# Inverse-transform tiles placed ahead of the last down products, and a planner's pacing table replaced

## The chip, the cores and the metric

The kernel runs on one core of one Trainium2 chip. Its time is the time of one execution in microseconds (us), as the device reports it. Engines are named as the profile names them: PE (matrix products), PEld (loads of the stationary operand), DVE, ACT, POOL (three elementwise engines) and SP (the queue that issues DMA transfers).

## The reference

The input `x` is 8192 tokens of 448 values. Every token is normalised, and the result is the input plus a spectral branch times a gate:

```python
xn = _layernorm(x, axis=-1)
s = _A_ref(xn, A_w1, A_b1, A_w2, A_b2)
g = _silu(_B_ref(xn, B_w_gate, B_w_up, B_w_down))
return x + s * g
```

`_A_ref` takes a real Fourier transform over the 8192 tokens, sends each frequency through a two-layer complex network in 4 blocks of 112 values (rectifier, soft threshold), and transforms back. `_B_ref` is a gated network: `(gelu(xn @ w_gate) * (xn @ w_up)) @ w_down` with 1792 hidden values.

## The kernel before

**Tiling.** Products are made of 16-bit high and low parts, three products for one, and are collected in PSUM banks (`bx`, `by`, and four shared `bd` banks). A token index is n = 64 n1 + n2, with n1 on the 128 partitions; a chunk is 4 values of n2, 512 tokens, and there are 16 chunks (`NG`), or 32 half chunks. The gated network runs twice over the chunks: pass 0 with hidden tiles 0 to 7, pass 1 with tiles 8 to 13. Pass 0 leaves its part of the down product in DRAM (`prt`), pass 1 adds its own to it. Most down products are made by `down2`, which turns eight block products into seven (`prod2`, numbered 1 to 7) with sums of weight blocks.

**Stages.** Phase 1 normalises, makes the weight parts and does the first stage of the forward transform; phase 2 does the second stage, the spectral network and the first inverse stage by groups of frequencies (`group`); phase 3 does the last inverse stage. The gated network runs beside all three, so PE always has products of both branches to mix. In phase 3 a half chunk `c` needs `u2` (columns of the inverse), `mt` (its matrix), `x2` (the input) and `g2` (the gate, written earlier to `gsp`). `load3` issues these loads on SP, `tiles3` makes the two tiles of 3 matmuls and 448 columns each, DVE multiplies bank and gate, and an addition of `x2` gives the output, which SP stores. For the last two half chunks (c = 30 and 31) the gate is not ready beforehand: their tiles are copied by ACT to `s4` (the profile calls it `s`), and the gate is applied in `ended2` and `last_half`, when the last down products are done: `Silu` on ACT into `th`, times `s4`, plus `x`, then the store. Chunks from `direct` on, except the last, take a middle way (`gate_bank`, `gate`).

**What sets the order.** The order on each engine is fixed when the program is built. The whole kernel is written as small tasks (Python generators); `Pace` advances a clock of its own, gives each instruction a cost on its engine, and starts the task that is next in time. So the order in which instructions stand depends on these costs. On the chip every engine then runs its instructions strictly in that order, waiting on semaphores where a producer on another engine is late.

`STEPS` is the planner's table: from the time in the first column on, the four others are the us added to a DMA's landing, how far ahead an engine may be booked before a task holds back (`clear`), a factor on the costs of all engines but PE, and a bias in the choice between two engines. `Either` makes that choice: `B` is DVE or POOL, `A` is ACT or POOL; the one that would end first by the plan is taken, with the bias added to POOL's end. The costs include that DVE and POOL can hold each other up (`shares`, `push_on`). `END3` is the planner's aim for the end of phase 3: half chunk number k of n3 starts its tiles at t0 + 10 + k (END3 - t0 - 12) / n3.

**What the change touches.** `Pace.note` (L151), which keeps the list of accesses that later instructions must wait for; the additions of `x` in `last_half` and `ended2`, both on DVE (`V`); `END3` in phase 2 and 3; and `STEPS`. All instructions are recorded through one helper, so the profile puts them all at L288.

Of the kernel before, what the change touches and what calls it, by code (L numbers as in the profile page):

```python
# [22 lines left out]
NG = 16  # L23
# [19 lines left out]
STEPS = ((0, 2.75, 0.05, 0.97, 0.0), (15, 2.75, 0.05, 0.97, 0.0), (25, 2.75, 0.05, 1.0, 0.3), (35, 2.75, 0.05, 1.0, 0.3), (45, 2.75, 0.05, 1.07, 0.0), (55, 2.75, 0.05, 1.07, 0.0), (65, 2.75, 0.05, 0.97, 0.0), (75, 2.75, 0.05, 0.97, 0.0), (87, 2.75, 0.15, 1.01, 0.0), (100, 2.75, 0.15, 1.01, 0.0), (125, 2.5, 0.15, 1.04, 0.0), (150, 2.5, 0.15, 1.04, 0.0), (175, 2.5, 0.15, 1.04, 0.0), (200, 2.5, 0.15, 1.04, 0.0), (225, 3.0, 0.15, 0.98, 0.0), (250, 2.75, 0.05, 1.0, 0.0), (275, 2.75, 0.05, 1.0, 0.0), (300, 2.75, 0.05, 1.0, 0.0), (325, 2.5, 0.05, 1.02, 0.0), (350, 2.5, 0.05, 1.02, 0.0), (375, 2.5, 0.05, 1.04, -0.3), (400, 2.5, 0.05, 1.04, -0.3), (425, 2.5, 0.05, 1.04, -0.3), (450, 2.5, 0.05, 1.04, -0.3), (475, 2.5, 0.05, 1.04, -0.3), (500, 2.5, 0.05, 1.04, -0.3), (525, 2.5, 0.05, 1.04, -0.3), (550, 2.5, 0.05, 1.04, -0.3), (575, 3.5, 0.05, 1.0, 0.0), (600, 3.5, 0.05, 1.0, 0.0), (625, 3.5, 0.05, 1.04, 0.0), (650, 3.5, 0.05, 1.04, 0.0), (675, 3.5, 0.05, 1.04, 0.0), (700, 3.5, 0.05, 1.04, 0.0), (725, 2.75, 0.05, 1.0, 0.0), (750, 2.75, 0.05, 1.0, 0.0), (775, 3.0, 0.05, 1.0, -0.3), (800, 3.0, 0.05, 1.0, -0.3), (825, 3.0, 0.05, 1.0, -0.5), (850, 3.0, 0.05, 1.0, -0.5), (875, 3.0, 0.05, 1.0, -0.5), (900, 3.0, 0.05, 1.0, -0.5), (925, 2.75, 0.05, 1.06, 0.0), (950, 2.75, 0.05, 1.06, 0.0), (975, 2.75, 0.05, 1.06, 0.0), (1000, 2.75, 0.05, 1.06, 0.0), (1025, 2.75, 0.05, 1.06, 0.0), (1050, 2.75, 0.05, 1.06, 0.0), (1075, 2.75, 0.05, 1.06, 0.1), (1100, 2.75, 0.05, 1.06, 0.1), (1125, 2.75, 0.05, 1.02, 0.0), (1150, 2.75, 0.05, 1.02, 0.0), (1175, 1.75, 0.05, 1.025, 0.0), (1200, 1.75, 0.05, 1.025, 0.0), (1225, 1.75, 0.05, 1.055, 0.0), (1250, 1.75, 0.05, 1.055, 0.0), (1275, 1.75, 0.05, 1.025, -0.2), (1300, 1.75, 0.05, 1.025, -0.2), (1325, 1.75, 0.05, 1.025, -0.2), (1350, 1.75, 0.05, 1.025, -0.2), (1375, 1.75, 0.05, 1.025, -0.4), (1400, 1.75, 0.05, 1.025, -0.4), (1425, 2.25, 0.1, 1.025, -0.4), (1450, 2.25, 0.1, 1.025, -0.4), (1475, 2.25, 0.1, 1.025, -0.4), (1500, 2.25, 0.1, 1.025, -0.4), (1525, 2.25, 0.1, 1.025, -0.4), (1550, 2.25, 0.1, 1.025, -0.4), (1575, 1.75, 0.1, 1.025, -0.4), (1600, 1.75, 0.1, 1.025, -0.4), (1625, 1.75, 0.1, 1.025, -0.4), (1650, 1.75, 0.1, 1.025, -0.4), (1675, 2.75, 0.05, 0.94, 0.1), (1700, 2.75, 0.05, 0.94, 0.1), (1725, 2.75, 0.05, 0.94, 0.4))  # L43
# [15 lines left out]
class Pace:  # L59
# [90 lines left out]
    def note(self, ap, write, t, e):  # L150
        name, lo, hi = self.region(ap)  # L151
        was = self.seen.setdefault(name, [])
        if write:
            was[:] = [x for x in was if not (lo <= x[0] and x[1] <= hi)]
        was.append([lo, hi, write, t, e])
        return was[-1]
# [399 lines left out]
def afno_geglu_kernel(ctx, tc, x, gu, raw, wd, mlp, b1, b2, c_m, c_mt, c_small, c_rows, out):  # L556
# [1222 lines left out]
    def last_half(i, qq, e, tf, a):  # L1779
# [13 lines left out]
        V.tensor_tensor(th, th, x4, op=ALU.add)  # L1793
# [3 lines left out]
    def ended2(p, i, qq, b, R, earlier=None):  # L1797
# [43 lines left out]
        V.tensor_tensor(th, th, x4, op=ALU.add)  # L1841
# [507 lines left out]
    def stores():  # L2349

        for g, (j0, m) in enumerate(GROUPS):
# [13 lines left out]

            pace.spawn(store())

    END1, END2, END3 = T1 + NG * DT + 12.0, 1450.0, 1730.0

    def phase2():  # L2370
        yield ev("phase1")
# [457 lines left out]
```

## Time and profile before

| | us |
|---|---|
| median of 3 runs | 1739.8 (1739.71 to 1740.24) |
| the profiled execution: its time | 1737.31 |
| its span, first to last instruction | 1735.5 |
| PE busy | 1709.6 of the span |
| DVE, ACT, POOL busy | 1404.9, 1097.0, 937.6 |
| start of PE's last matmuls (21 in 4.13 us) | 1721.74 |
| last DMA issue | 1731.80 |

In the rows of the profile, `bd<-u,mt` is a tile of the last inverse stage; `bd<-dw,h`, `bd<-wt,h`, `bd<-dw,wt` and the same into `by` or `bx` are down products; `g<-bd,ms,g` multiplies a bank and a gate, `g<-g,x` adds the input. A row of a timeline has the start, the time to the end, engine, line, operation, operands and count; in brackets stands the idle time of the engine before it and what ended it. A row of groups has the sum of busy time and the mean of one in ns. Matmuls overlap in the pipeline: 12 of 224 columns take 1.31 us together, though one alone is shown with about 0.26 us.

### The profile page before, as it was taken

Reading aid. Unit: us, or ns where it says so; the run is one execution under the profiler, and the core shown is the slowest. Engines: PE = TensorE matmul, PEld = TensorE weight load, DVE = VectorE, ACT = ScalarE, POOL = GpSimd, SP = SyncE. Lnnn points to the kernel's source line nnn. Section 1 sums busy time; section 2 is a strip of 40 time slices with the busy share of each in tenths; the row PEclk is TensorE's granted clock in tenths of the full one; section 3 lists DMA queues with packets and bytes.
Section 4 is the critical chain, followed back from the end, with each engine's and each line's share of the span. In section 5 each row is a group of like instructions: output and inputs, shape, how many; then the busy total and the mean of one; then the engine's idle time right before and its main releaser. Section 6 shows DMA issues by size and latency. Waiting matters only on the chain.

```text
span 1735.5 us, 40997 instructions
## 1 busy us (share of the span) xinstructions
PE 1709.6 (99%) x15654; PEld 1434.6 (83%) x15654; DVE 1404.9 (81%) x2438; ACT 1097.0 (63%) x2240; POOL 937.6 (54%) x1291
## 2 busy tenths in 40 slices
PE   9999999999999999999999999999999999999997
PEld 4447677766777999998989999999999999889886
DVE  8999888878885778778777788888888787687787
ACT  6767666757675556678776667666766676333333
POOL 3467666667565574457566454355445454344442
PEclk9999999999999999999999999999999999999999
DMA  7448987878858543254346865544556455999987
GB/s 265 149 135 252 270 254 221 288 206 229 237 163 242 149 124 74 60 127 106 92 111 185 210 163 131 120 120 104 131 139 145 113 134 113 293 287 306 303 288 257
DMA packets 438310, 316.63 MB, mean 182 GB/s; under 512 B 305793, under 2 KB 409601, under 8 KB 436321
## 3 DMA queue, kind: packets, MB, share of 16 engines
q1 hardware_dynamic: 437824, 313.99, 64.6%
q8 instruction: 122, 2.00, 0.5%
q14 instruction: 76, 0.61, 0.1%
q10 hardware_dynamic: 288, 0.03, 0.0%
HBM read 137.93 MB, written 108.25 MB: 142 GB/s over the span
## 4 chain that ended last, share of the span: by engine, by line
PE 44%; DVE 3%; POOL 2%; ACT 1%; issue 1%; SPq 0%; DMA 0%; DVEq 0%; ACTq 0%; POOLq 0%
PE bd L288 19%; PE bx L288 14%; PE by L288 11%; DVE wt L288 1%; DVE th L288 0%; POOL wn L288 0%; POOL h L288 0%; DVE va L288 0%; POOL wt L288 0%; DVE h L288 0%; SPq L288 0%; DVE g L288 0%; ACT h L288 0%; DVE o L288 0%; DVE t L288 0%
## 5 line engine op out<-in xcount | busy, mean ns | idle before, releaser
L288 PEld LDWEIGHTS <-wt 128*128 128x128 f16 x9142 | 884.6, 98 | 160.3 <-issue 9.5
L288 PE MATMUL bx<-xta,wt 128*128 128x256 f16 (+1 forms) x2819 | 354.7, 275 | 2.2 <-ACT by L288 1.3
L288 PEld LDWEIGHTS <-h 128*128 128x128 f16 x2711 | 259.6, 98 | 76.3 <-POOL h L288 1.1
L288 PE MATMUL by<-xtb,wt 128*128 128x256 f16 x2080 | 255.2, 273 | 0.6 <-DVE by L288 0.6
L288 PE MATMUL bd<-dw,h 128*128 128x448 f16 (+1 forms) x1536 | 241.3, 306 | 0.4 <-DVE ysb L288 0.4
L288 POOL TENSOR_TENSOR wt<-wt 128x256 f32<-128x256 f32 x133 | 107.2, 806 | 158.8 <-DVE wt L288 151.5
L288 PE MATMUL bx<-xtb,wt 128*128 128x256 f16 x1248 | 153.3, 273 | 0.0
L288 PE MATMUL by<-xta,wt 128*128 128x256 f16 (+1 forms) x899 | 123.9, 282 | 0.7 <-DVE u L288 0.5
L288 DVE TENSOR_TENSOR by<-bx,u 128x512 f32<-128x512 f32 x104 | 72.2, 695 | 40.4 <-PE bx L288 34.8
L288 ACT ACTIVATE u<-by,fc 128x512 f32<-128x512 f32 (+1 forms) x118 | 73.4, 635 | 49.1 <-PE by L288 47.4
L288 PE MATMUL bx<-left,wt 128*128 128x256 f16 x816 | 99.9, 273 | 1.0 <-ACT by L288 1.0
L288 PE MATMUL bd<-dw,wt 128*128 128x224 f16 (+1 forms) x816 | 97.9, 264 | 1.4 <-DVE left L288 1.4
L288 POOL TENSOR_TENSOR t<-h 112x256 f32<-112x256 f32 (+1 forms) x34 | 26.0, 765 | 125.8 <-ACT h L288 104.9
L288 ACT COPY u<-by 128x512 f32<-128x512 f32 x104 | 60.7, 584 | 49.2 <-PE by L288 49.1
L288 ACT CAST h<-wt 128x512 f16<-128x512 f32 (+1 forms) x128 | 68.4, 535 | 34.0 <-DVE wt L288 28.9
L288 DVE SCALAR_TENSOR_TENSOR left<-bd,ms,left 128x448 f32<-128x448 f32 x96 | 64.3, 680 | 27.1 <-PE bd L288 26.6
L288 DVE TENSOR_TENSOR v<-bx,u 128x512 f32<-128x512 f32 x104 | 71.2, 685 | 16.6 <-PE bx L288 15.9
L288 POOL TENSOR_TENSOR h<-wt,h 128x256 f16<-128x256 f32 (+1 forms) x65 | 71.4, 1106 | 15.5 <-ACT h L288 15.4
L288 PE MATMUL bd<-w2t,wn 113*128 113x112 f16 (+1 forms) x1152 | 78.3, 212 | 0.9 <-DVE bd L288 0.6
L288 ACT COPY by<-bx 128x512 f32<-128x512 f32 x104 | 60.0, 577 | 24.8 <-PE bx L288 24.3
L288 PE MATMUL bd<-wt,h 128*128 128x224 f16 x603 | 72.9, 259 | 0.6 <-POOL h L288 0.5
L288 PEld LDWEIGHTS <-wn 113*128 113x128 f16 (+1 forms) x1152 | 69.3, 97 | 4.1 <-issue 1.2
(280 smaller groups left out, 3801.8 us busy)
## 6 DMA issues: line engine op xcount, KB each, us to landing
xts<-sx SPq DMA_DIRECT2D x32, 480.0 KB, 4.1
x<-in_x SPq DMA_DIRECT2D x17, 896.0 KB, 6.9
t<-ysb SPq DMA_DIRECT2D x64, 224.0 KB, 3.8
prt<-th SPq DMA_DIRECT2D x64, 224.0 KB, 3.3
vt<-va SPq DMA_DIRECT2D x256, 56.0 KB, 2.1
left<-prt SPq DMA_DIRECT2D x64, 224.0 KB, 3.8
u<-t SPq DMA_DIRECT2D x32, 448.0 KB, 6.0
x<-in_x SPq DMA_DIRECT2D x32, 448.0 KB, 6.4
```

The costliest lines, as they stand in the source:

```text
L288: return self.pace.issue(self.name, kind, out, ins, lambda: fn(out, *args, **kw))
```

## The change

Four edits. `STEPS` is another table of 75 rows. `END3` goes from 1730 to 1716, so the last half chunks are planned up to 14 us earlier. The additions of `x` in `last_half` and `ended2` go to DVE or POOL, whichever ends first by the plan. And `note` drops an older read of the same stretch by PE when PE reads it again.

```diff
-STEPS = ((0, 2.75, 0.05, 0.97, 0.0), (15, 2.75, 0.05, 0.97, 0.0), (25, 2.75, 0.05, 1.0, 0.3),
+STEPS = ((0, 2.75, 0.05, 1.0, 0.0), (15, 2.75, 0.05, 1.0, 0.0), (25, 2.75, 0.3, 1.0, 0.8),
...
         if write:
             was[:] = [x for x in was if not (lo <= x[0] and x[1] <= hi)]
+        elif e == "PE":
+            was[:] = [x for x in was if x[4] != e or x[2] or x[0] != lo or x[1] != hi]
         was.append([lo, hi, write, t, e])
...
-        V.tensor_tensor(th, th, x4, op=ALU.add)
+        B.tensor_add(th, th, x4)
         yield
         Q.dma_start(blk(ov[:, CH * i:CH * i + CH, :], *qq)[:, v], th)
...
-        V.tensor_tensor(th, th, x4, op=ALU.add)
+        B.tensor_add(th, th, x4)
         PT.put(q)
...
-    END1, END2, END3 = T1 + NG * DT + 12.0, 1450.0, 1730.0
+    END1, END2, END3 = T1 + NG * DT + 12.0, 1450.0, 1716.0
```

Both programs have the same 15654 matmuls, of the same shapes, and the same number and shapes of DMAs; their order differs, and 44 elementwise instructions more stand on POOL, 42 fewer on DVE and 2 fewer on ACT. Of the instructions `wt<-wt,wt` (128x512), for example, DVE had 42 and POOL 22, and now they have 28 and 36. The helper's line is L290 in the changed kernel.

**The end of PE's list.** The last down product is the one into `bx`. Before, seven tiles of the inverse (each 3 matmuls, shown by one) stand behind it: `u_24554` and `u_24606` are half chunks 30 and 31, `u_24325` and `u_24503` two earlier ones.

```order
L288 MATMUL bx<-wt_80,h 128x224
...
L288 MATMUL bd_66<-u_24554,mt 128x448
...
L288 MATMUL bd_69<-u_24325,mt 128x448
...
L288 MATMUL bd_67<-u_24554,mt 128x448
...
L288 MATMUL bd_66<-u_24606,mt 128x448
...
L288 MATMUL bd_69<-u_24606,mt 128x448
...
L288 MATMUL bd_67<-u_24503,mt 128x448
...
L288 MATMUL bd_66<-u_24503,mt 128x448
```

Now `u_24528` and `u_24575` are half chunks 30 and 31, and `u_24345` is the last of the others; the rows from product 6 of `down2` on (`bd_69<-wt_78,h`), one row for each run of equal kind:

```order
L290 MATMUL bd_67<-u_24236,mt 128x448
...
L290 MATMUL bd_66<-u_24528,mt 128x448
...
L290 MATMUL bd_67<-u_24528,mt 128x448
...
L290 MATMUL bd_69<-wt_78,h 128x224
...
L290 MATMUL bd_66<-u_24575,mt 128x448
...
L290 MATMUL bd_67<-u_24575,mt 128x448
...
L290 MATMUL bd_66<-u_24345,mt 128x448
...
L290 MATMUL bd_69<-wt_80,h 128x224
...
L290 MATMUL bx<-wt_80,h 128x224
...
L290 MATMUL bd_67<-u_24345,mt 128x448
```

Six of the seven tiles have moved in among the last down products, three of them in one run ahead of the end of product 6; one stays behind the last down product.

**The end of the elementwise lists.** Before, DVE's last rows, from the addition of the last half down product (`left<-bx`) on; POOL has one addition (`g_24551`) in this stretch, and none behind it:

```order
L288 SCALAR_TENSOR_TENSOR left<-bx,ms,left 128x224
L288 SCALAR_TENSOR_TENSOR g_24551<-bd_69,ms,g_24551 128x448
L288 TENSOR_TENSOR g_24551<-g_24551,x_24507 128x448
L288 TENSOR_TENSOR th<-th,s_21491 128x448
L288 TENSOR_TENSOR th<-th,x_24209 128x448
...
L288 SCALAR_TENSOR_TENSOR g_24683<-bd_67,ms,g_24683 128x448
...
L288 TENSOR_TENSOR th<-th,x_24558 128x224
L288 TENSOR_TENSOR g_24683<-g_24683,x_24610 128x448
...
L288 SCALAR_TENSOR_TENSOR g_24683<-bd_66,ms,g_24683 128x448
```

Now DVE's rows from the same addition on, and then POOL's last ones:

```order
L290 SCALAR_TENSOR_TENSOR left<-bx,ms,left 128x224
L290 TENSOR_TENSOR th<-th,s_21492 128x448
L290 TENSOR_TENSOR th<-th,s_21492 128x224
L290 SCALAR_TENSOR_TENSOR g_24581<-bd_67,ms,g_24581 128x448
L290 TENSOR_TENSOR g_24581<-g_24581,x_24579 128x448
```

```order
L290 TENSOR_TENSOR th<-th,x_24532 128x448
L290 TENSOR_TENSOR g_24581<-g_24581,x_24579 128x448
L290 TENSOR_TENSOR th<-th,x_24240 128x448
L290 TENSOR_TENSOR th<-th,x_24532 128x224 x2
```

Behind `left<-bx` DVE had 16 instructions and now has five (the product `th<-th,s` of 128x224 stands there twice, with `g_24581<-bd_67` between); four of the five additions into `th` at the end have gone to POOL.

**DVE in phase 1.** Here DVE frees the bank `by` for PE with `u<-by,fc,u`. Before, the rows between two of these instructions, and then now:

```order
L288 SCALAR_TENSOR_TENSOR dw_85<-xtb,fd,dw_84 128x448
L288 SCALAR_TENSOR_TENSOR raws<-raws,rowc 128x128
L288 BN_STATS st<-x_411 128x6
L288 BN_AGGR st<-st 128x2
L288 SCALAR_TENSOR_TENSOR dw_85<-wo,fd,dw_84 128x448
L288 SCALAR_TENSOR_TENSOR u_992<-by,fc,u_992 128x512
```

```order
L290 SCALAR_TENSOR_TENSOR dw_85<-xtb,fd,dw_84 128x448
L290 SCALAR_TENSOR_TENSOR raws<-raws,rowc 128x128
L290 SCALAR_TENSOR_TENSOR u_988<-by,fc,u_988 128x512
L290 BN_STATS st<-x_401 128x6
L290 BN_AGGR st<-st 128x2
L290 SCALAR_TENSOR_TENSOR dw_85<-wo,fd,dw_84 128x448
```

A pair of statistics and one `dw` have moved from ahead of `u` to behind it.

2 lines of the change are left out of this document (1 added, 1 removed).

## The prediction, made before the changed kernel ran

> **What bounds the kernel now.** The page comes first: the share of each engine.
>
> ```profile
> span 1735.5 us, 40997 instructions
> PE 1709.6 (99%) x15654; PEld 1434.6 (83%) x15654; DVE 1404.9 (81%) x2438; ACT 1097.0 (63%) x2240; POOL 937.6 (54%) x1291
> ```
>
> PE is busy for all but 26 us of the span, and both programs have the same 15654 matmuls, so the change can only act on those 26 us. The view by windows tells where they lie; of its 21 rows, those with 2 us or more of idle PE, three of the last stage, and the sum.
>
> ```profile
> 0.00:100.00 100.00, 95.10 (x483) 45.04 (x484) 89.22 (x177) 64.33 (x138) 43.32 (x68) 1.00 0.52 183
> 100.00:200.00 100.00, 97.79 (x640) 62.19 (x639) 91.45 (x174) 73.49 (x151) 73.36 (x130) 1.00 0.80 230
> 200.00:300.00 100.00, 97.59 (x770) 74.73 (x769) 88.85 (x153) 67.89 (x135) 65.82 (x115) 1.00 0.83 249
> 800.00:900.00 100.00, 97.61 (x1045) 89.70 (x1044) 79.60 (x129) 75.19 (x164) 67.26 (x78) 1.00 0.47 111
> 1600.00:1650.00 50.00, 50.00 (x457) 44.09 (x456) 37.13 (x53) 18.95 (x34) 21.67 (x25) 1.00 0.98 314
> 1650.00:1700.00 50.00, 49.95 (x458) 44.32 (x457) 40.57 (x59) 18.89 (x33) 21.71 (x22) 1.00 0.91 298
> 1700.00:1736.00 36.00, 24.54 (x212) 20.02 (x209) 27.63 (x49) 11.38 (x21) 8.45 (x8) 0.93 0.65 230
> sum 1736.00, PE 1709.56 PEld 1434.59 DVE 1404.88 ACT 1096.98 POOL 937.64; mean PE 81.41 PEld 68.31 DVE 66.90 ACT 52.24 POOL 44.65
> ```
>
> The last 36 us hold 36.00 - 24.54 = 11.5 us without PE; all before them hold 1700 - (1709.56 - 24.54) = 15.0 us, of which 4.9 + 2.2 + 2.4 in the first 300 us. In between PE's granted clock is 1.00 and it hardly waits. So two things are worth reading: the end, and single waits. The end, from PE's, DVE's and SP's timelines:
>
> ```profile
> 1712.63 1.31 PE L288 MATMUL bd<-dw,wt 128*128 128x224 f16 x12 [0.59 <-DVE left L288]
> 1714.59 1.13 PE L288 MATMUL bd<-wt,h 128*128 128x224 f16 x10 [0.46 <-POOL h L288]
> 1716.01 1.31 PE L288 MATMUL bd<-dw,wt 128*128 128x224 f16 x12 [0.29 <-DVE left L288]
> 1721.46 0.45 PE L288 MATMUL bx<-wt,h 128*128 128x224 f16 x3
> 1721.74 4.13 PE L288 MATMUL bd<-u,mt 128*128 128x448 f16 x21
> 1721.95 0.45 DVE L288 SCALAR_TENSOR_TENSOR left<-bx,ms,left 128x224 f32<-128x224 f32 x1 [0.18 <-PE bx L288]
> 1724.88 0.63 DVE L288 TENSOR_TENSOR th<-th,s 128x448 f32<-128x448 f32 x1 [0.46 <-ACT s L288]
> 1730.02 0.68 DVE L288 SCALAR_TENSOR_TENSOR g<-bd,ms,g 128x448 f32<-128x448 f32 x1
> 1731.15 0.62 DVE L288 TENSOR_TENSOR g<-g,x 128x448 f32<-128x448 f32 x1
> 1731.80 0.36 SPq L288 DMA_DIRECT2D out<-g  x1
> ```
>
> The last down product ends at about 1721.9 (1721.46 + 0.45). Behind it PE makes seven tiles until 1725.87 (1721.74 + 4.13). The gate of the last chunk needs four of them (`s`), so its products start at 1724.88 only, and from there DVE runs without a break until 1731.77; the last store is issued at 1731.80 and the span ends 3.7 us after DVE, at 1735.5. **After PE's last matmul come 9.6 us** in which DVE's list is what ends last.
>
> **The change part by part.** The sum is made against the profiled execution, 1737.31 us (span 1735.5 and 1.8 around it), 2.5 us below the median of the runs, 1739.8; I carry that 2.5 over.
>
> *The six tiles.* They are 18 matmuls of (4.13 - 0.35) / 20 = 0.19 us (0.35 is one alone), 3.4 us. They leave the place behind the last down product and stand ahead of it: PE does the same work in total, so its last matmul stays at 1725.87 unless waits change. What moves is DVE: it had 16 instructions behind `left<-bx` and now has five. One tile (0.57 us) stays, so `left<-bx` starts about 0.4 us before PE's last matmul ends, and PE ends 0.74 us after the last down product. DVE then has its 0.45, three `th` products and the two of `g`; the price of the `th` products by width and of the additions on POOL:
>
> ```profile
> L288 DVE TENSOR_TENSOR th<-th,s 128x224 f32<-128x224 f32 x2 | 0.8, 383 | 0.0
> L288 POOL TENSOR_TENSOR th<-th,x 128x448 f32<-128x448 f32 x5 | 6.1, 1212 | 25.2 <-DVE th L288 25.2
> L288 POOL TENSOR_TENSOR wt<-wt 128x256 f32<-128x256 f32 x62 | 50.4, 813 | 80.0 <-DVE wt L288 76.6
> ```
>
> Alone, DVE's five take 0.63 + 0.38 + 0.68 + 0.38 + 0.62 = 2.7 us; from 0.6 us behind the last down product that ends 3.3 us behind it, 2.6 us behind PE, and with the 3.7 us of store 6.3 us: the lower bound. But two of POOL's last three additions, about 0.75 us each at 224 columns (between 1.21 for 448 and 0.81 for 256), and one of 1.2, stand beside them, and DVE and POOL do hold each other up:
>
> ```profile
> 1610.93 1.15 POOL L288 TENSOR_TENSOR wt<-wt,wt 128x512 f16<-128x512 f32 x1
> 1611.03 2.07 DVE L288 TENSOR_TENSOR g<-g,x 128x448 f32<-128x448 f32 x2
> ```
>
> Two additions of 0.62 took 2.07 us on DVE, beginning while POOL was at work: the first waited until POOL was done. If DVE and POOL take turns for all of these, DVE's second `th` product waits for the whole 1.2 of POOL's addition, and the last two 224-wide additions and products wait for each other by about 0.4 more, the rest passing beside `g<-bd`: 1.6 us later, 7.9 us after PE, the upper bound. I take 7.0, about the middle, since both the free runs of DVE at 1724 to 1731 and the held one at 1611 are rows of this stage. **Gain 9.6 - 7.0 = 2.6 us** (1.7 to 3.3).
>
> [...]
>
> *PE's waits ahead of it.* Three waits near the end sum to 0.59 + 0.46 + 0.29 = 1.3 us. Three tiles (1.7 us of PE) now stand ahead of the place where PE waited for POOL's `h`, which covers its 0.46. The tile that stood ahead of the first wait is gone, so that wait can grow by 0.57, if DVE, which runs `left` in the same list, is as late as before. **Gain 0.2 us** (0.9 lost to 0.9 gained).
>
> *The additions on DVE or POOL elsewhere* in phase 3 cost nothing: PE never waited for one there (50.00 and 49.95 of 50 us busy).
>
> *The table, phase 1.* A wait and the DVE rows ahead of it:
>
> ```profile
> 92.32 0.62 DVE L288 BATCH_NORM_STATS2 st<-x 128x6 f32<-128x448 f32 x1
> 93.07 0.94 DVE L288 SCALAR_TENSOR_TENSOR dw<-wo,fd,dw 128x448 f16<-128x448 f32 x1
> 93.94 0.74 DVE L288 SCALAR_TENSOR_TENSOR u<-by,fc,u 128x512 f32<-128x512 f32 x1
> 94.73 1.46 PE L288 MATMUL by<-wt,wt 128*128 128x512 f16 x6 [1.46 <-DVE u L288]
> ```
>
> PE waited 1.46 us for `u`. The pair of statistics and the `dw` that ran from 92.32 to 93.94 now stand behind `u`: 1.62 us less ahead of it. **Gain 1.3 us** (0 if the next user of DVE is late instead, at most 1.46).
>
> *The table, the largest wait.*
>
> ```profile
> 272.21 3.42 DVE L288 SCALAR_TENSOR_TENSOR wst<-wst,rowc 128x128 f32<-128x128 f32 x1
> 275.56 1.07 DVE L288 SCALAR_TENSOR_TENSOR gl<-v,fc,gl 128x256 f32<-128x256 f32 x2
> 276.88 0.17 PE L288 MATMUL bd<-ident,mxr 2*128 2x2 bf16 x1 [1.81 <-DVE mxr L288]
> ...
> L288 DVE TENSOR_TENSOR wo<-wst,wo 128x256 f16<-128x256 f32 x14 | 13.4, 957 | 0.0
> ```
>
> PE waited 1.81 us for a small maximum (`mxr`) because DVE was held for 3.42 us in an instruction on 128 columns; from there to the end of `gl` DVE took 4.4 us. In the new order other DVE work lies between the same two points: `wo<-wst,wo` (256 columns), `gl`, a pair of statistics, `ysb` (448 columns out of a bank) and `u`. By rows of their kinds: 0.4 (0.62 of 448 columns, by width) to 0.96, 0.74 as `u`, 0.75 (92.32 to 93.07), 0.68 as `g<-bd`, 0.74; together 3.3 to 3.9. **Gain 0.7 us** (0 to 1.2).
>
> *The rest of the waits*, 15.0 - 1.46 - 1.81 = 11.7 us before 1700, 3.4 of them (4.9 - 1.46) in the first 100 us, where PE's list begins as before. The other 8.3 are dealt anew by a table that changes the order nearly everywhere. Bounds: all 8.3 gone, or as many again added. I take nothing: no row says which. The edit in `note` drops an older read by PE where a newer one on the same stretch is kept; what has to be waited for stays the newest, so it costs nothing.
>
> Sum: 2.6 + 0.2 + 1.3 + 0.7 = 4.8 us. 1737.3 - 4.8 = 1732.5 for a profiled execution, and 1739.8 - 4.8 = **1735.0** for the median.
>
> **The rivals.** *The rest of the waits shrinks as well.* For it: they are single waits where one engine was 0.5 to 2 us late, and a new order has no reason to be late at the same places. Against it: it can be late at others. With 5 of the 8.3 us gone: 1730.
>
> *The end gives the gain back through the loads.* The DMA share is 0.98 at 1600 and 0.91 after; tiles that stand 3.4 us earlier on PE need their loads as much earlier. Issue to landing in the last 300 us, and the longest wait for a load there:
>
> ```profile
> u<-t SPq DMA_DIRECT2D x32, 448.0 KB, 6.0
> g<-gsp SPq DMA_DIRECT2D x22, 448.0 KB, 5.5
> ...
> POOL g L288 <- DMA g<-gsp: 8.5, 1, 8.5
> ```
>
> SP issues in order, and the load for half chunk 31 (`u_24575`) stands behind two stores of `th` that now wait for POOL. If it comes when it did before relative to the span, PE waits in front of the last down products for up to 3.4 us and the end gains nothing; with the two waits of phase 1 kept, 1738. Against it: PE is not in that list with any of these loads, and the share falls to 0.65 in the last 36 us, so 12 us of transfers have room.
>
> *POOL becomes late in phases 2 and 3 (slower).* The 44 instructions more on POOL are mostly differences that PE needs next, `wt<-wt,wt` first (22 before, 36 now):
>
> ```profile
> L288 POOL TENSOR_TENSOR wt<-wt,wt 128x512 f16<-128x512 f32 x22 | 27.3, 1239 | 10.6 <-ACT wt L288 10.4
> L288 DVE TENSOR_TENSOR wt<-wt,wt 128x512 f16<-128x512 f32 x42 | 35.4, 844 | 1.3 <-ACT wt L288 1.1
> ```
>
> Each takes 0.4 us longer there and holds DVE meanwhile. If PE waits 0.6 us (the 0.46 that it waited for POOL's `h`, a little more) at each of the 14, 8.4 us are lost: 1735.0 + 8.4 = 1743.4. It decides from the point where POOL has more to do than the time between two of these, and POOL's 54% speaks against that.
>
> **How the numbers follow.** Chances: the forecast 0.48 (its own range 1731.5 to 1738), the rest shrinks as well 0.22, the loads give it back 0.20, POOL late 0.10. Nothing under 0.2% (3.5 us) can be told from no change here: faster is under 1736.3, slower over 1743.3. Faster: 0.40 of the forecast, all of the second, 0.02 of the third: 0.64. Slower: 0.07 of POOL late and 0.01 of the loads: 0.08. The rest, 0.28, is the same. The range goes from 1727.5 (the second rival and 2.5 us of the waits more) to 1741.5 (into the last two), and leaves out about 0.05 below and 0.13 above.
>
> **What would show it.** In the changed profile: PE's last matmul within 1.5 us of 1725.9 less what waits were saved; 6.3 to 7.9 us between it and the span's end, with a store of `g` or of a 224-wide `th` last; POOL's `th<-th,x` at 1.2 us and DVE's stretched beside them; no wait of PE for `u` near 94; under 1.4 us for `mxr` near 290; no `PE bd <- DMA u` in the list of waits. It is wrong if PE's idle time before 1700 is far from 15.0 - 2.0 us, or if a load ends a wait of PE in the last 40 us.

## The result, and the profile of the changed kernel

| kernel | median us | runs us | ratio to before, 95% interval |
|---|---|---|---|
| before | 1740.02 | 1739.71 to 1742.28 (4) | |
| changed | 1731.24 | 1729.34 to 1732.78 (4) | 0.9946 [0.9929, 0.9963] |

The changed kernel is 8.8 us faster; the forecast was 4.8. The profiled execution is the one of 1732.78 us, the slowest of its four. Its page begins with the span and the busy shares:

```profile
span 1730.7 us, 40922 instructions
PE 1710.0 (99%) x15654; PEld 1434.9 (83%) x15654; DVE 1373.7 (79%) x2396; ACT 1101.2 (64%) x2238; POOL 962.8 (56%) x1335
```

PE's busy time is the same 1710 us; in this pair all of the difference is time in which PE stands idle, and time behind its last matmul. The view by windows, of the changed kernel: stretch, its length, busy us of PE, PEld, DVE, ACT and POOL, granted clock, DMA share, GB/s.

```profile
0.00:300.00 300.00, 291.42 (x1892) 182.94 (x1893) 261.72 (x495) 205.71 (x420) 184.06 (x313) 0.99 0.70 216
300.00:1700.00 1400.00, 1396.50 (x13573) 1233.68 (x13571) 1089.29 (x1870) 885.18 (x1800) 760.42 (x1005) 1.00 0.65 175
1700.00:1731.00 31.00, 22.14 (x195) 18.24 (x192) 22.74 (x34) 10.30 (x18) 18.30 (x18) 0.92 0.56 199
```

Idle PE is 8.6 us in the first 300 (9.5 before), 3.5 in the next 1400 (5.4 before), 8.9 in the rest (11.5 before). The end, from the timelines of PE, DVE, POOL and SP (start, length, engine, operation, count, and in brackets the idle time ahead of it and what ended it):

```profile
1712.86 0.73 PE L290 MATMUL bd<-u,mt 128*128 128x448 f16 x3 [0.21 <-DVE g L290]
1714.83 1.13 PE L290 MATMUL bd<-wt,h 128*128 128x224 f16 x10 [1.04 <-DVE h L290]
1716.16 0.74 PE L290 MATMUL bd<-dw,wt 128*128 128x224 f16 x6 [0.20 <-DVE left L290]
...
1722.79 0.45 PE L290 MATMUL bx<-wt,h 128*128 128x224 f16 x3
1723.08 0.73 PE L290 MATMUL bd<-u,mt 128*128 128x448 f16 x3
...
1712.06 2.17 POOL L290 TENSOR_TENSOR h<-wt,h 128x512 f16<-128x512 f32 x2
1713.62 1.15 DVE L290 TENSOR_TENSOR h<-wt,h 128x512 f16<-128x512 f32 x1
...
1723.28 0.45 DVE L290 SCALAR_TENSOR_TENSOR left<-bx,ms,left 128x224 f32<-128x224 f32 x1 [0.18 <-PE bx L290]
1723.65 0.92 DVE L290 TENSOR_TENSOR th<-th,s 128x448 f32<-128x448 f32 x2
1724.48 0.68 DVE L290 SCALAR_TENSOR_TENSOR g<-bd,ms,g 128x448 f32<-128x448 f32 x1
1725.08 0.72 DVE L290 TENSOR_TENSOR th<-th,s 128x224 f32<-128x224 f32 x1
1725.72 1.07 DVE L290 TENSOR_TENSOR g<-g,x 128x448 f32<-128x448 f32 x1
...
1724.39 2.91 POOL L290 TENSOR_TENSOR th<-th,x 128x448 f32<-128x448 f32 x3 [0.86 <-POOL g L290]
...
1727.34 0.33 SPq L290 DMA_DIRECT2D out<-th  x1
```

One tile stands behind the last down product, and PE ends at 1723.81 (1723.08 + 0.73). From there to the end of the span it is 6.9 us, against 9.6 before. DVE's list behind `left<-bx` is down to five instructions, and what now ends last is POOL: its three additions end at 1727.30, and the last store, of `th`, is issued at 1727.34. The holds between the two engines are to be seen in the lengths: 0.72 for a product that took 0.38 alone, 1.07 for the addition that took 0.62.

### The profile page after: what moved, and what is told of

The parts are those of the page before. It is cut to its first block, busy times and chain, and to the rows that moved or that the text cites. A ratio compares the mean times of both kernels' runs of the same rounds, so it can differ in the third digit from the quotient of the medians.

```text
span 1730.7 us, 40922 instructions
## 1 busy us (share of the span) xinstructions
PE 1710.0 (99%) x15654; PEld 1434.9 (83%) x15654; DVE 1373.7 (79%) x2396; ACT 1101.2 (64%) x2238; POOL 962.8 (56%) x1335
## 4 chain that ended last, share of the span: by engine, by line
PE 89%; DVE 5%; POOL 2%; issue 1%; ACT 1%; DMA 1%; SPq 0%; POOLq 0%; DVEq 0%; ACTq 0%
PE bd L290 36%; PE bx L290 31%; PE by L290 23%; DVE wt L290 1%; POOL wt L290 1%; DVE h L290 1%; POOL st L290 0%; DMA m<-c_m 0%; POOL h L290 0%; SPq L290 0%; DMA raws<-in_gu 0%; DVE xs L290 0%; POOL wo L290 0%; DMA xts<-xs 0%; ACT x L290 0%
## 5 line engine op out<-in xcount | busy, mean ns | idle before, releaser
L290 PEld LDWEIGHTS <-wt 128*128 128x128 f16 x9142 | 885.0, 98 | 159.5 <-issue 8.7
L290 PE MATMUL bx<-xta,wt 128*128 128x256 f16 (+1 forms) x2819 | 355.2, 276 | 2.0 <-ACT by L290 1.0
L290 PEld LDWEIGHTS <-h 128*128 128x128 f16 x2711 | 259.7, 98 | 77.2 <-DVE h L290 1.3
L290 PE MATMUL by<-xtb,wt 128*128 128x256 f16 x2080 | 254.4, 272 | 0.6 <-DVE by L290 0.3
L290 PE MATMUL bd<-dw,h 128*128 128x448 f16 (+1 forms) x1536 | 242.8, 306 | 0.0
L290 POOL TENSOR_TENSOR wt<-wt 128x256 f32<-128x256 f32 x137 | 110.7, 808 | 140.4 <-DVE wt L290 130.9
L290 PE MATMUL bx<-xtb,wt 128*128 128x256 f16 x1248 | 153.2, 273 | 2.8 <-DVE v L290 2.7
L290 PE MATMUL by<-xta,wt 128*128 128x256 f16 (+1 forms) x899 | 124.5, 283 | 0.2
L290 ACT ACTIVATE u<-by,fc 128x512 f32<-128x512 f32 (+1 forms) x118 | 73.5, 635 | 56.2 <-PE by L290 54.7
L290 DVE TENSOR_TENSOR by<-bx,u 128x512 f32<-128x512 f32 x104 | 72.3, 696 | 43.0 <-PE bx L290 38.0
L290 PE MATMUL bx<-left,wt 128*128 128x256 f16 x816 | 99.6, 273 | 0.0
L290 PE MATMUL bd<-dw,wt 128*128 128x224 f16 (+1 forms) x816 | 98.4, 264 | 0.4 <-DVE left L290 0.4
L290 POOL TENSOR_TENSOR h<-wt,h 128x256 f16<-128x256 f32 (+1 forms) x74 | 80.5, 1096 | 31.1 <-ACT h L290 28.1
L290 ACT COPY u<-by 128x512 f32<-128x512 f32 x104 | 60.8, 584 | 48.1 <-PE by L290 47.2
L290 DVE TENSOR_TENSOR v<-bx,u 128x512 f32<-128x512 f32 x104 | 71.4, 687 | 23.4 <-PE bx L290 22.3
L290 ACT CAST h<-wt 128x512 f16<-128x512 f32 (+1 forms) x128 | 68.3, 535 | 33.2 <-DVE wt L290 25.9
L290 DVE SCALAR_TENSOR_TENSOR left<-bd,ms,left 128x448 f32<-128x448 f32 x96 | 64.3, 679 | 26.8 <-PE bd L290 26.5
L290 PE MATMUL bd<-w2t,wn 113*128 113x112 f16 (+1 forms) x1152 | 78.1, 212 | 0.8 <-DVE u L290 0.4
L290 POOL TENSOR_TENSOR t<-h 112x256 f32<-112x256 f32 (+1 forms) x34 | 26.4, 776 | 89.9 <-ACT h L290 87.1
L290 PE MATMUL bd<-wt,h 128*128 128x224 f16 x603 | 73.0, 259 | 1.3 <-DVE h L290 1.0
L290 DVE SCALAR_TENSOR_TENSOR u<-by,fc,u 128x512 f32<-128x512 f32 (+1 forms) x86 | 55.3, 657 | 22.6 <-PE by L290 16.3
L290 PEld LDWEIGHTS <-wn 113*128 113x128 f16 (+1 forms) x1152 | 69.3, 97 | 3.9 <-issue 0.6
```

The costliest lines, as they stand in the source:

```text
L290: return self.pace.issue(self.name, kind, out, ins, lambda: fn(out, *args, **kw))
```

## The experiments

Two questions were open: which of the edits carries the gain, and why 8.8 us and not 4.8. The theory of the prediction was that the end carries half of it (2.6 of 4.8) and two waits in phase 1 the rest. The first rival was that the new order sheds waits all along the list; another, that one execution differs from the next by more than the terms of the sum, so that a pair of profiles tells little. Three series were run, each beside the kernel before.

| series, kernel | median us | runs us | ratio to before, 95% interval |
|---|---|---|---|
| 1 before | 1738.47 | 1737.6 to 1741.13 (11) | |
| 1 changed, again | 1730.32 | 1727.92 to 1733.76 (5) | 0.9955 [0.9942, 0.9967] |
| 1 additions on DVE | 1733.95 | 1731.96 to 1736.04 (7) | 0.9974 [0.9963, 0.9985] |
| 1 END3 at 1730 | 1731.94 | 1730.38 to 1732.3 (5) | 0.9960 [0.9946, 0.9974] |
| 1 edits with the old table | 1743.83 | 1742.35 to 1749.26 (5) | 1.0037 [1.0024, 1.0049] |
| 2 before | 1739.60 | 1736.48 to 1741.8 (15) | |
| 2 before, again | 1739.23 | 1737.88 to 1742.08 (11) | 1.0000 [0.9992, 1.0009] |
| 2 new table without the other edits | 1732.88 | 1731.79 to 1733.22 (5) | 0.9956 [0.9943, 0.9968] |
| 2 new table up to t=275 only | 1752.04 | 1749.6 to 1755.01 (5) | 1.0065 [1.0052, 1.0079] |
| 2 changed, END3 at 1722 | 1728.23 | 1727.9 to 1730.63 (5) | 0.9933 [0.9921, 0.9945] |
| 3 before | 1739.05 | 1738.17 to 1740.85 (9) | |
| 3 changed, third time | 1729.10 | 1727.85 to 1732.75 (5) | 0.9943 [0.9931, 0.9956] |
| 3 POOL later near 152 | 1729.16 | 1728.28 to 1731.3 (5) | 0.9944 [0.9930, 0.9958] |
| 3 END3 at 1722, again | 1731.46 | 1727.61 to 1732.48 (5) | 0.9950 [0.9938, 0.9963] |
| 3 END3 at 1722 and POOL later | 1728.76 | 1727.37 to 1731.2 (5) | 0.9940 [0.9928, 0.9953] |

### Both kernels again, unchanged

Expected of the changed kernel, and then of the kernel before:

> The changed kernel once more. Theory (the sum of waits at the end and in phase 1, made against one profiled execution each): profiled spans fell by 4.8 us (1735.5 to 1730.7), so the medians should fall by 4.8 too, to about 1735. Rival: the profiled execution of before was 2.5 us below its median and the one of the changed kernel 1.5 us above its own, so single executions differ by some us in PE's waits and the medians differ by 8 to 9 us again (ratio 0.995); then this profile shows a span under 1730 with waits missing that the first one had.

> The kernel before, unchanged, for a second profiled execution. Theory A (waits of PE are fixed by the order of the lists): the same waits return, 1.46 us for u near 94, 1.81 for mxr near 277, 2.4 us without PE between 800 and 900, and the profiled execution stands 2 to 2.5 us below the median as the first did. Theory B (one execution differs from the next by who of DVE and POOL starts first): the single waits are there or not from one execution to the next, each worth 1 to 3.5 us, and the profiled execution lies anywhere within the spread of the runs, 1737.5 to 1741. Both: 9.6 us after PE's last matmul, since no wait between engines there depends on what happened before. Time 1739 by both.

The view by windows: two rows of the first profile of the kernel before, two of its second, and two of the second of the changed kernel.

```profile
0.00:300.00 300.00, 290.47 (x1889) 181.96 (x1890) 269.52 (x502) 205.72 (x422) 182.51 (x313) 1.00 0.71 221
300.00:1700.00 1400.00, 1394.55 (x13557) 1232.61 (x13556) 1107.74 (x1888) 879.88 (x1798) 746.68 (x970) 1.00 0.64 173
```

```profile
0.00:300.00 300.00, 287.81 (x1871) 180.56 (x1872) 268.67 (x497) 204.62 (x420) 182.65 (x312) 0.99 0.70 219
300.00:1700.00 1400.00, 1394.54 (x13550) 1231.84 (x13549) 1109.73 (x1892) 879.62 (x1800) 748.40 (x971) 1.00 0.64 173
```

```profile
0.00:300.00 300.00, 294.75 (x1918) 184.92 (x1919) 261.84 (x500) 208.39 (x424) 189.40 (x326) 1.00 0.72 220
300.00:1700.00 1400.00, 1396.47 (x13588) 1235.38 (x13587) 1090.45 (x1870) 883.46 (x1799) 760.78 (x998) 1.00 0.65 175
```

The changed kernel is 8.2 us faster again, as its rival had it, and the second profile of the kernel before lies above its median (1740.35 and 1739.23), where the first lay 2.5 us below. Read by columns, PE's idle time behind the first 300 us belongs mostly to the kernel: 5.45 and 5.46 us before, 3.50 and 3.53 changed, 3.89 in a third profile of the changed kernel, taken later. In the first 300 us it belongs to the execution too: 9.5 and 12.2 before, 8.6, 5.3 and, in the third profile, 6.0 changed. So both theories of the repeated kernel before are right, each in its part of the program. Which waits recur is told by PE's timeline; of the second profile of the kernel before:

```profile
94.84 1.67 PE L288 MATMUL by<-wt,wt 128*128 128x512 f16 x7 [1.46 <-DVE u L288]
279.82 0.17 PE L288 MATMUL bd<-ident,mxr 2*128 2x2 bf16 x1 [1.81 <-DVE mxr L288]
```

The waits of 1.46 and 1.81 us are the same to the hundredth, 0.1 and 2.9 us later. One thing that differs lies near 154 us. DVE's and POOL's timelines at the same place, in the first profile of the kernel before, in its second, in the first of the changed kernel and in its second:

```profile
154.17 0.42 DVE L288 TENSOR_TENSOR wt<-raws,wt 128x256 f16<-128x256 f32 x1
154.42 2.01 POOL L288 TENSOR_TENSOR wt<-raws,wt 128x256 f16<-128x256 f32 x3 [0.49 <-ACT wt L288]
```

```profile
154.06 2.72 DVE L288 TENSOR_TENSOR wt<-raws,wt 128x256 f16<-128x256 f32 x1
154.19 1.68 POOL L288 TENSOR_TENSOR wt<-raws,wt 128x256 f16<-128x256 f32 x3
155.83 0.66 POOL L288 TENSOR_TENSOR sx<-sf,sx 128x256 f16<-128x256 f32 x1
```

```profile
154.00 2.72 DVE L290 TENSOR_TENSOR wt<-raws,wt 128x256 f16<-128x256 f32 x1
154.13 1.68 POOL L290 TENSOR_TENSOR wt<-raws,wt 128x256 f16<-128x256 f32 x3
```

```profile
152.32 0.41 DVE L290 TENSOR_TENSOR wt<-raws,wt 128x256 f16<-128x256 f32 x1
152.56 2.01 POOL L290 TENSOR_TENSOR wt<-raws,wt 128x256 f16<-128x256 f32 x3 [0.41 <-ACT wt L290]
```

The same DVE instruction took 0.42 and 0.41 us where POOL came 0.25 and 0.24 us behind it, and 2.72 both times where POOL came 0.13 behind it: in the second profile of the kernel before it ended 0.3 us after POOL's four instructions in a row (1.68 and 0.66 us, to 156.5; DVE's ends at 156.8). An execution is called held or free here by this instruction. The kinds of the two instructions are the same in all four, and DVE starts ahead of POOL in all four: in these rows neither the kind nor the order of the recorded starts tells the held from the free.

The hold is not all that differs. All executions of a kernel run the same lists, so the start of each matmul in one can be set against its start in the other. The second execution of the kernel before ends up 2.9 us behind the first: 1.2 near 158, where PE waits 1.05 us for `v` behind the hold (0.2 of it is made up again), and 1.8 between 220 and 224, where DVE has waited 2.15 us for the load of `wmx` instead of 1.10. The first execution of the changed kernel ends up 4.9 us behind its second: 0.2 by 19 us, 1.6 between 19 and 22, 1.2 near 156 behind the hold, and 1.8 between 165 and 175. In the 1.6 us PE is not idle (4.62 of the 5.00 us around them are busy, as in the first profile of the kernel before); the granted clock is 0.66, where that one has 1.00. The window of that stretch and seven matmuls in it, first profile and then, of the same matmuls, second:

```profile
19.00:24.00 5.00, 4.62 (x26) 3.16 (x26) 4.53 (x11) 3.06 (x7) 0.00 (x0) 0.66 1.02 369
20.64 1.70 PE L290 MATMUL by<-xta,wt 128*128 128x256 f16 x7
```

```profile
19.93 0.92 PE L290 MATMUL by<-xta,wt 128*128 128x256 f16 x7
```

In the second profile the granted clock of this window is 1.00. Nor is all idle time lost time: of the 2.7 us between 9.5 and 12.2, 1.4 are a longer wait for the load of `m` (0.39 and 1.76 us) that ends at the same 9.4 to 9.5 us in both executions.

So the first profile of the kernel before was a free execution, and the first of the changed kernel a held one that lost 1.6 us to the clock as well. The pair compared for the result differs by 4.5 us (1737.31 to 1732.78); held against held it is 7.6 (1740.35 to 1732.78), or 9.2 without the 1.6 of the clock; free against free 9.4 (1737.31 to 1727.92). The medians, 8.8 us apart at first and then 8.2 and 10.0 in the two series that ran both, go with these last ones.

### The last additions back on DVE

```
-        B.tensor_add(th, th, x4)
+        V.tensor_tensor(th, th, x4, op=ALU.add)
```

> The changed kernel with the last additions of x back on DVE; PE's order is the same. Theory that DVE and POOL take turns: the additions on POOL cost about 0.8 us of held DVE, so on DVE alone the end stays within 0.6 us of the changed kernel (time after PE's last matmul 6.5 to 7.5 us). Rival, that both work at the same time: four additions (2 x 0.62 + 2 x 0.39) come on top of DVE's list and the end is 1.4 to 2 us later.

1733.95, 3.6 us slower than the changed kernel beside it. In the profile, DVE's and POOL's timelines behind the last down product, PE having ended at 1722.94:

```profile
1724.78 1.62 DVE L290 TENSOR_TENSOR th<-th,s 128x224 f32<-128x224 f32 x2
1726.32 1.22 DVE L290 TENSOR_TENSOR th<-th,x 128x448 f32<-128x448 f32 x3
...
1724.94 1.21 POOL L290 TENSOR_TENSOR g<-g,x 128x448 f32<-128x448 f32 x1 [2.84 <-DVE g L290]
```

From PE's end to the span's it is 9.0 us against 6.9, so the additions on POOL are worth 2.1 us at the end (the rest of the 3.6 us is within the spread of the runs). Taking turns was expected to leave 0 to 0.6; 2.1 is near what the rival had, with both engines at work at once. Of these 2.1, 0.9 arise ahead of the last three additions: DVE has a fourth one at 1721.41, held for 1.18 us, and `left<-bx` starts 0.35 us behind PE's end (1723.29) where it started 0.53 ahead of it. The hold is there too, with the places changed: two DVE products of 0.38 took 1.62 beside POOL's `g<-g,x`.

### END3 back at 1730

```
-    END1, END2, END3 = T1 + NG * DT + 12.0, 1450.0, 1716.0
+    END1, END2, END3 = T1 + NG * DT + 12.0, 1450.0, 1730.0
```

> The changed kernel with END3 back at 1730; PE's order is the same up to the first tiles of phase 3 and six of the last seven tiles still stand ahead of the last down product. Theory that the place of the tiles makes the gain at the end: DVE has 8 instructions behind the last half addition (4.3 us) instead of five, so 8.2 us come after PE's last matmul instead of 6.9, 1.3 us slower than the changed kernel. Rival, that END3 itself carries the 2.6 us: 2.5 us or more slower.

1731.94, 1.6 us slower than the changed kernel beside it, and 8.3 us behind PE's end, near the 8.2 of the theory. All but one of the tiles still stand ahead of the last down product; so with the new table they stand there without END3 at 1716, which only spaces them. With the old table END3 at 1716 brings them ahead too, as the next run shows.

### All edits with the old table

```
-STEPS = ((0, 2.75, 0.05, 1.0, 0.0), (15, 2.75, 0.05, 1.0, 0.0), (25, 2.75, 0.3, 1.0, 0.8),
+STEPS = ((0, 2.75, 0.05, 0.97, 0.0), (15, 2.75, 0.05, 0.97, 0.0), (25, 2.75, 0.05, 1.0, 0.3),
...
```

> All edits with the table of before: PE's order is that of before up to phase 3, and no tile stands behind the last down product; nine tiles stand in one run ahead of it. Theory: the waits before phase 3 are those of before, 5.5 us come after PE's last matmul instead of 9.6, so 4 us faster than before if the loads are in time. Rival: the run of tiles comes 3.4 us or more earlier than its loads, PE waits for u or mt there, and the gain is 0 to 2 us.

1743.83: 5.4 us slower than before, where neither theory had a loss. Here the rival of the prediction on the loads is at work. From SP's and PE's timelines of the profiled execution, the slowest of the five (1749.26):

```profile
1727.46 0.34 SPq L290 DMA_DIRECT2D out<-g  x1
1728.33 0.67 SPq L290 DMA_DIRECT2D mt<-c_mt  x1
...
1726.41 2.44 PE L290 MATMUL bd<-u,mt 128*128 128x448 f16 x12 [1.08 <-DMA mt<-c_mt]
1732.77 4.13 PE L290 MATMUL bd<-u,mt 128*128 128x448 f16 x18 [3.91 <-DMA mt<-c_mt]
```

With the old table and the limit of 1716, tiles of 36 matmuls (6, 12 and 18, parted by the waits alone) stand in one run ahead of the last down products. The load for the last of them stands on SP behind a store of `g` that is issued at 1727.46 only; it follows at 1728.33, and PE waits 3.91 us for it. In the changed kernel none of PE's waits near the end is for a load. Behind PE's last matmul come 7.8 us, not the 5.5 expected.

Not all that this execution lost is the loads'. Up to 1597 us the lists of PE, DVE, ACT and POOL are those of the kernel before, row for row, and there it already lies 6.1 us behind the first profile of the kernel before; 4.8 of the 10.9 us between the two spans come later. One of the waits ahead of 1597 is 3.46 us for `fx` near 278. The same lists gave 0.39 there in both profiles of the kernel before, and the 1.81 for `mxr` behind it; here DVE was held in `fx` (3.20 us), one instruction earlier, and there is no wait for `mxr`.

### The new table without the other edits

```
-        B.tensor_add(th, th, x4)
+        V.tensor_tensor(th, th, x4, op=ALU.add)
...
-    END1, END2, END3 = T1 + NG * DT + 12.0, 1450.0, 1716.0
+    END1, END2, END3 = T1 + NG * DT + 12.0, 1450.0, 1730.0
```

> The changed kernel with the last additions back on DVE and the limit END3 back at 1730; the new table stays. From the runs so far: additions 2.1 us at the end (9.0 us after PE against 6.9), END3 1.4 us (8.3 against 6.9). Theory A (the two act on the same 2.7 us, DVE's list behind the last down product): together at most 9.6 us after PE, 1733 to 1734. Theory B (they add): 10.4 after PE, 1734.5. Either way the table alone is worth what is left against 1739: 5 to 6 us, most of it in waits before 1100.

1732.88, 6.7 us faster than before: the table carries most of the gain. The edit in `note` stays in this run. It has no part in the order ahead of phase 3: with it and the old table (the run above) the lists are those of the kernel before up to 1597 us, and without it (the run below) the table's early entries alone give the lists of the changed kernel up to 281 us. What `note` does behind that was not tried alone. The end is 8.3 us behind PE's last matmul (1722.92 to 1731.2), as with END3 at 1730 and POOL's additions. With this END3, then, it is of no matter where the additions run. DVE's timeline shows why:

```profile
1725.09 1.22 DVE L290 TENSOR_TENSOR th<-th,x 128x448 f32<-128x448 f32 x3
1726.82 0.63 DVE L290 TENSOR_TENSOR th<-th,s 128x448 f32<-128x448 f32 x1 [0.51 <-ACT th L290]
```

DVE has done all else and waits 0.51 us for ACT's last `th`. The two edits do not add (10.4 us was theory B): undone together they lengthen the end by 1.4 us, where one of them alone does it by 1.4 or 2.1. Each needs the other: POOL's additions shorten a list that ends last only with END3 at 1716.

### The new table in phase 1 only

```
-(25, 2.75, 0.05, 1.0, 0.3)
+(25, 2.75, 0.3, 1.0, 0.8)
...
```

That is the kernel before, with the entries of the new table for t below 275.

> The kernel before with the new table's entries up to t=275 only; everything behind is paced by the old entries. Theory A (the waits near 94 and 277 are undone by the new order in phase 1, the first 300 us): 2.0 us less as the terms of the prediction have it, 3 to 4 by the profile of the changed kernel's second execution; 1735 to 1737, with 9 to 10 us after PE's last matmul. Theory B (the gain of the table is in the later phases): 1738 to 1740.

1752.04, 12.4 us slower than before, outside both theories. By windows:

```profile
0.00:300.00 300.00, 291.44 (x1903) 183.23 (x1904) 264.02 (x497) 206.31 (x421) 186.01 (x317) 1.00 0.71 218
300.00:1700.00 1400.00, 1380.44 (x13405) 1217.48 (x13403) 1111.62 (x1860) 870.89 (x1782) 758.31 (x986) 1.00 0.63 171
```

In the first 300 us it does what the changed kernel does: 8.6 us idle, to the tenth the 8.6 of the changed kernel's first profile, and a held execution like it. Behind them PE idles 19.6 us, where the kernel before has 5.4. The list of the later phases was dealt anew as well, since the planner goes on from another state; the waits are spread over all of it, the longest 1.97 us near 1357. Why the old entries do so much worse from that state is not shown. That the effect of phase 1 can be had alone is so neither shown nor refuted for the sum; the windows show that it is there.

### END3 at 1722

```
-    END1, END2, END3 = T1 + NG * DT + 12.0, 1450.0, 1716.0
+    END1, END2, END3 = T1 + NG * DT + 12.0, 1450.0, 1722.0
```

> The changed kernel with END3 at 1722, between its 1716 and the 1730 of before. The list then has no tile behind the last down product and the tiles before it stand wider apart. Theory A (what lies behind the last down product is DVE's list and nothing else): five to six tenths of a us less behind PE's last down product, 6.3 to 6.9 us after PE's end, and 0.5 to 1.5 us faster than the changed kernel, 1729 to 1730, if the last loads are in time. Theory B (the load of half chunk 31 was in time by less than 0.1 us in the changed kernel, and tiles that stand no later wait for it): a wait of PE for u or mt of 0.5 to 2 us near the end and 1731 to 1732.

> The changed kernel with END3 at 1722 again, now beside the changed kernel. Theory A (no tile behind the last down product and wider spacing are worth 0.7 us behind PE's end, with loads in time): 0.5 to 1.5 us faster than the changed kernel beside it, near 1729. Theory B (its 1728.2 against 1730.3 in another series was the hold near 152 us, which its profiled execution did not have): as fast as the changed kernel beside it within 0.5 us.

No tile stands behind the last down product, and 6.2 us lie behind PE's end (1719.59 + 0.45 to 1726.2) instead of 6.9; in place of that, two waits for `h` near the end sum to 1.3 us, the larger for ACT:

```profile
1711.22 0.37 PE L290 MATMUL bd<-wt,h 128*128 128x224 f16 x2 [0.88 <-ACT h L290]
1712.03 1.13 PE L290 MATMUL bd<-wt,h 128*128 128x224 f16 x10 [0.45 <-DVE h L290]
```

The changed kernel had 1.04 at that `h`. In one series its median is the lowest of all, 1728.23; in the next it is 1731.46, beside 1729.10 of the changed kernel. No gain over the changed kernel is shown: what a tail of 0.7 us less is worth lies below the spread of the executions.

### POOL later near 152 us

```
             if self.name == "POOL":
+                self.calls = self.calls + 1
+                if self.calls == 142:
+                    for _ in range(3):
+                        self.engine.memset(PAD[0], 0.0)
```

> The changed kernel once more, as the base of the three runs beside it. Theory A (who of DVE and POOL starts first near 152 us decides about 3 us of waits for v and by between 155 and 180, and it falls either way): the runs spread over 1727.5 to 1734 with the median at 1730 to 1731, and the profiled execution has either 0.5 or 3.5 to 4 us of such waits, as the two before. Theory B (the difference of those two profiles was something that drifts over the whole span): waits in between, at other places too.

> The changed kernel with three idle POOL instructions (about 0.1 us each) just ahead of POOL's first wt<-raws,wt of 152 us; every other list stays row for row. In the profiles of the changed kernel and of the kernels with its table, POOL's instruction began 0.13 us behind DVE's wt<-raws,wt in the held cases (DVE 2.72 us) and 0.14 to 0.26 behind it in the free ones (0.41). Theory A (DVE and POOL take turns there, and the first one has it): DVE is always first now, its instruction takes 0.4 us, no wait of 1.2 us for v at 155 to 160, 1728 to 1729.5 with a narrower spread, if about half of the executions of the changed kernel were held. Theory B (the hold has another cause): DVE still takes 2.7 us in some profiles and the median stays at 1730 to 1731.

> Both edits: END3 at 1722 and POOL 0.3 us later near 152 us. If the two act at different places and add: 1727 to 1728.5, the fastest of the four, with a spread under 3 us. If one of them does nothing, the time of the other alone.

The changed kernel came out at 1729.10, below the 1730 to 1731 expected, and its profile was a free one. DVE's and POOL's timelines of the first of the two kernels with the delay, at the place of the hold:

```profile
152.08 0.41 DVE L299 TENSOR_TENSOR wt<-raws,wt 128x256 f16<-128x256 f32 x1
152.19 0.41 POOL L298 MEMSET pad<- 128x4 f32 x3
152.60 1.89 POOL L299 TENSOR_TENSOR wt<-raws,wt 128x256 f16<-128x256 f32 x3
```

DVE's instruction is free in both profiles with the delay (0.41 us, POOL 0.52 behind it). In the twelve without it, it was free in six and held for 2.72 in six; POOL was 0.13 us behind it in all of the held, and 0.14 once and 0.16 to 0.26 five times in the free. In four of these five POOL waited for ACT's `wt`. That agrees with theory A, but two profiles settle little: of the eight in which POOL did not wait for ACT six were held, and at that rate two free ones come by chance once in 16 times. And the time does not show it: 1729.16 beside 1729.10, a spread of 3.0 us beside 4.9. One reason is to be seen. The profile of END3 at 1722 in the third series is free at 152 and still has 2.4 us of waits for `v`, as the list of waits says; that stretch has more than one such meeting of DVE and POOL, and the delay takes out one. Near 174 us DVE's `sf<-x,sf` takes 1.31 us there, beside POOL's `h<-u,h`, where the second profile of the changed kernel has 0.35. The same profile also lost 1.6 us near 20 us; the granted clock of its first 300 us was 0.99, against 1.00 in the changed kernel's second profile.

```profile
PE bx L290 <- DVE v L290: 2.4, 3, 1.3
```

The two edits together gave 1728.76, just outside the 1727 to 1728.5 expected: not to be told from 1729.10 either.

## Why the prediction was right, and where not

**The end** was right in mechanism and size: 9.6 to 6.9 us, where 7.0 was forecast, with the store of a 224-wide `th` last. Two of DVE's five instructions were held, 0.72 us instead of 0.38 and 1.07 instead of 0.62: a hold of 0.8, half of the 1.6 of the upper bound. But the prediction had DVE's list end last, and POOL's ends 0.5 us behind it (1727.30 and 1726.79): its three additions took 2.91 us where the prices of the prediction make 2.7. That 7.0, the middle of the bounds, was met so closely is in part luck. With DVE and POOL taking turns, as the upper bound had it, the additions on POOL were expected to gain 0 to 0.6 us; measured, they are worth 2.1 us. What the prediction did not have is which edit does it. The new table is enough to place the tiles; with it alone the end is 8.3, and only POOL's additions together with END3 bring the other 1.4.

**PE's waits ahead of it**: 0.2 gained was forecast; 0.3 was lost, inside the bounds. The first wait, 0.59, is 0.22, another of 0.21 is new. But the wait for `h`, 0.46, is 1.04 in spite of three tiles ahead of it. The step had the tiles cover POOL's `h`. Now the wait ends with DVE's piece of `h`, which stands behind `g<-g,x` and beside POOL's two (2.17 us from 1712.06): it takes 1.15 us, where DVE's `h<-u,h` of the same shape took 0.68 near 158. The cover was reckoned for the engine that was late, and did not hold for the one that was late next.

**The wait for `u`** is gone, as forecast (1.3 us); a new one of 0.32 us at 83 takes a little back, so that 1.1 are gained.

**The largest wait** was mis-sized: the 1.81 us for `mxr` near 277 are gone, 1.8 gained where 0.7 was taken and 1.2 was the upper bound. The step summed the DVE work that now lies between the two points, as if the hold had a price to be replaced. What made the wait was the hold itself, 3.42 us in a scaling of 128 columns. In the new order the same instruction stands beside POOL's `wst<-wst`, which starts 0.03 us ahead of it, and took 0.57 us; DVE's and POOL's timelines of the changed kernel's second profile:

```profile
276.28 0.57 DVE L290 SCALAR_TENSOR_TENSOR wst<-wst,rowc 128x128 f32<-128x128 f32 x1
276.25 2.52 POOL L290 TENSOR_TENSOR wst<-wst 64x128 f32<-64x128 f32 x4
```

All ten profiles with the whole new table have 0.56 or 0.57 us for it. Why it is not held there is not shown.

**The rest of the waits** is the step that failed in size. It was taken as 0 ± 8.3 us for what is left between 100 and 1700 us. Free against free, 5.6 of these 8.3 us remain: 2.7 gained. Behind 300 us the gain is 1.9 us (5.45 to 3.53): the waits of 1.1 near 822, 1.0 near 1021 and 0.5 near 389 are gone, and one for POOL's `xs` near 475 is new, the largest in the list of waits of the changed kernel's second profile (sum, times, longest), in which the 0.4 for `mxr` is the one near 19 us that the kernel before has too (0.38):

```profile
PE bd L290 <- POOL xs L290: 1.6, 1, 1.6
...
PE bd L290 <- DVE mxr L290: 0.4, 1, 0.4
```

All ten profiles with the whole new table have 3.4 to 4.3 us behind 300, those of the kernel before and of the edits with the old table 5.4 to 6.2. In the first 300 us the idle time falls by 4.3 us free against free (9.53 to 5.25) and by 3.6 held against held (12.19 to 8.58), where the two terms of phase 1 made 2.0 (measured 1.1 + 1.8). The prediction's own sign of being wrong, an idle time before 1700 far from 13.0 us, shows in the free executions: 8.8 and 9.9 us; the held first one has 12.1.

**The base.** "2.5 us below the median of the runs ... I carry that 2.5 over" treats the distance of one profile from its median as a constant of the kernel. It holds for the free executions (the changed kernel's second profile lies 2.4 us below its median), but not from one execution to the next: the second profile of the kernel before lies 1.1 above its median. Free against free, the idle times measure 4.3 + 1.9 + 2.7 - 0.3 = 8.6 us, and the two executions are 9.4 apart; PE's busy time, 1709.6 and 1708.6, makes the better part of the rest. The sum of 4.8 was too small by nearly half. It lay near the first pair of profiles (4.5) by luck, because the first execution of the changed kernel was held (1.2 us behind the hold, 1.8 behind later meetings) and had lost 1.6 us to the clock.

**The rivals.** The first, that the rest shrinks as well, at 1730, came nearest: 1731.24 lies just outside the likeliest case's own range of 1731.5 to 1738, and its chance of 0.22 was too low. In size it was helped by luck: it had 5 of the 8.3 us gone, and 2.7 went; the largest wait gave 1.1 more than its term. Its argument held, that waits do not return at the same places; so did the one against it, since new ones came. The second, the loads, is no part of the changed kernel, but it is real: with the old table PE waits 5.0 us for `mt`. The third, POOL late: POOL does make PE wait where it did not, 1.6 us near 475, but for `xs` and not for `wt<-wt,wt`, and once, not 14 times.

## What to carry to other kernels

Take two profiles of the kernel before a sum is made against one, and set them matmul against matmul: what recurs can be costed, the rest is the spread of the executions, and the pair must be of the same kind, its granted clock included (0.66 against 1.00 near 20 us went with 1.6 us here). Two are few: here 0.39 us for `fx` and 1.81 for `mxr` recurred to the hundredth, and a third profile of the same lists had 3.46 and nothing. Where a planner deals an order from a table, the table is one piece: half of the new one cost 12 us, the other edits without it 5, the whole gained 9. A long stretch of DVE in a short instruction was no price here: the same instruction took 2.72 us or 0.41 near 154, beside POOL both times, and another 3.42 in the first profile of the kernel before and 0.56 or 0.57 in all with the new table. When the order changes, let the bounds reach to all of such a stretch, since that one went whole.

## What the hardware showed that was not expected

A DVE difference (`wt<-raws,wt`, 0.41 us when free) was held not for one POOL instruction but through four in a row, 2.3 us, while POOL took 1.68 us for the first three and 0.66 for the fourth (256 columns each), although DVE's recorded start lies ahead of POOL's. In the changed kernel's second profile, a free one, the other instructions at this place took longer on both engines than in its first, a held one: POOL's three 2.01 instead of 1.68 us, and DVE's next two 0.82 and 0.64 instead of 0.35 and 0.41. In the seven profiles with POOL's start 0.13 or 0.14 us behind DVE's in the record, DVE was held in six and free in one; in the seven with POOL 0.16 to 0.52 us behind, it was free in all.

The granted clock of a short stretch near 20 us was not the same in two executions of the same program (0.66 and 1.00 in the windows of the changed kernel's first and second profile, 19 to 24 us). The same seven matmuls took 1.70 us and 0.92 there, and by 22 us the first lay 1.6 us further behind.
